# Sharing out the float64 weight roundings and the length-64 transforms over the first five channel pairs of a Fourier filter and mixer kernel

## The chip, the cores and the metric

The kernel runs on one core of one Trainium2 chip. The metric is the device time of one execution in microseconds (us), lower is better. The time of the kernel before is the median of three runs. All durations come from one profiled execution, which has its own time.

## What is computed

For a batch of 8 sequences of 3008 tokens with 256 channels, a filter in the frequency domain is followed by an MLP mixer block. Cut to what matters:

```python
X = np.fft.rfft(x, axis=1)                       # x: (8, 3008, 256)
y = np.fft.irfft(X * (filt_r + 1j * filt_i), n=3008, axis=1).astype(np.float32)
h = np.maximum(y.transpose(0, 2, 1) @ w_tok1, 0.0) @ w_tok2    # 3008 -> 256 -> 3008
u = y + h.transpose(0, 2, 1)
out = u + np.maximum(u @ w_ch1, 0.0) @ w_ch2                   # 256 -> 1536 -> 256
```

The four weight matrices arrive as float64, so the kernel rounds them to float32 itself, on the chip.

## The kernel before, in words

**The filter.** 3008 is 47 times 64. A Fourier transform of a batch is a transform of length 64 over one index (`a_unit`, one matmul of a 128x512 tile, two passes in the trace; `a_pair` with halves from the third group on) whose result goes to DRAM as z (`z_out`, L515: a ScalarE copy out of PSUM, L517, into one of two t1 buffers, and a DMA, L519), then for each of 32 frequencies a transform of length 47, the product with the filter, and the transform back (`b_pair`, `join`, `bi_pair`, L638 to L660), whose result goes to DRAM as g. The function `dft` (L535) is a generator: it works for one group of batches and stops (`yield`) after each piece. The groups are batch 0, batches 1 and 2, 3 and 4, 5 and 6, and 7. At the change from length 64 to length 47 it clears three filter tiles on GpSimd (`memset`, L664), and for the first two of 16 frequency pairs loads z back into t2 (`t2_load`, L591, on SP's DMA queue) and a table wb and the filter rows (`w_load`, L550, nine DMAs on SP's queue, L548, L215 and L217).

**The mixer.** `token_sums` and `token_relu` make the token mixer's hidden layer of a batch; `u_part` makes u for one of six tiles of 512 tokens. For each tile, `mix` (L954) loops over six channel pairs: 256 of the 1536 hidden channels. A pair's two matrix products are split into seven smaller ones each (the numbers n = 0 to 6 in the weight tiles), with sums of operands before and after. One pass i of the loop holds the first layer of pair i and the second layer of pair i-1:

- `up_first` (L840): four matmuls into PSUM (L844), a ScalarE copy into s (L847); `up_middle` (L850): two DVE adds that read that PSUM (output hh and s);
- `h_sums` of pair i-1: DVE (output t); `down` part 0: three matmuls (L878);
- the first place (`yield b, i % n, 0`);
- `up_last` (L856): three matmuls (L860) into the same PSUM banks, then two times a DVE add into hh and a ScalarE ReLU (L865);
- the second place; `down` part 1: four matmuls (L878); pieces of the next u; the third place.

Every DVE sum of the mixer carries line L822, that of the helper `v`. Both first-layer PSUM banks are used again by the next pair, so its `up_first` follows this pair's hidden adds.

At each place the loop at L1109 may advance the filter's generator of the group after this one; before the change, in group 0, it takes one piece at every place (three length-64 units a pair).

**The rounding.** A weight tile is one of 38 generators in the list `tiles`: 12 for w_tok1, 14 for w_tok2, 2 first and then 10 more for w_ch1 and w_ch2 (`LAST`, L395: c2_0, c1_1, c1_4, c2_1, c1_2, c2_2, c1_5, c2_3, c2_4, c2_5, where c1 and c2 mean `wc1_load` and `wc2_load`). Each has four steps:

1. begin: a staging tile st and its load, issued on GpSimd (L372: four DMAs; L383: one);
2. copy: ScalarE writes the upper word's float into "top" (L265);
3. middle: two DVE instructions on top (L267, L268);
4. end: two DVE instructions make "rest" (L271, L273), one or two add top and rest into the weight tile wc (L295); then `combine` (L359) makes the sums of weights, five GpSimd instructions for a pair (L362 to L366).

```python
def convert_end():
    ended[0] += 1
    advance(end)
    copies()
    fill(5)
...
    while copied[0] < len(tiles) and copied[0] <= ended[0] + (copied[0] < len(tiles) - len(LAST)):
```

`advance(it)` takes the next tile of an iterator and runs its next step. `convert` is `convert_middle` and `convert_end`. For the last ten tiles top is a tile of pool p1 and rest one of pool p2, one buffer each, so the copy of a tile follows the end of the one before it. In `mix` (L987 and L1008) there is one `convert` at the head of a pass and one after its first place. So in passes 0 to 4 the order on DVE in each half is: end of one tile, middle of the next, then the mixer's adds of that half.

**The tail.** `finish` adds up a token tile, transposes it on DVE (L910) and writes it with 16 DMAs from `store` (L925), on GpSimd's queue, but for the very last tile on three queues in turn.

Of the kernel before, what the change touches and what calls it, by code (L numbers as in the profile page):

```python
# [10 lines left out]
FP32 = mybir.dt.float32  # L11
# [12 lines left out]
P = 128  # L24
# [17 lines left out]
JP = JT // 2  # L42
# [77 lines left out]
def kernel(  # L120
# [11 lines left out]
    nc = tc.nc  # L132
# [145 lines left out]
    def spare_pair():  # L278
# [2 lines left out]
        both = where.tile([P, 2, 512], FP32, tag=tag, name="both")  # L281
        return both[:, 0], both[:, 1]

    def rounded(st, n, parts, late):
        if late:

            pair = (p1p.tile([P, 512], FP32, tag="p1", name="top"), p2p.tile([P, 512], FP32, tag="p2", name="rest"))
        else:
            pair = spare_pair()
        h = halves(st, n, pair)  # L290
        yield next(h)
        yield next(h)
        top, rest = next(h)
        for src, dst in parts:
            nc.vector.tensor_tensor(out=dst, in0=src(top), in1=src(rest), op=ALU.add)  # L295
# [115 lines left out]
    def convert():  # L411

        convert_middle()
        convert_end()

    def convert_middle():
        advance(middle)
        sum_up()

    def convert_end():  # L420
        ended[0] += 1
        advance(end)
        copies()
        fill(5)

    copied = [0]

    def copies():

        while copied[0] < len(tiles) and copied[0] <= ended[0] + (copied[0] < len(tiles) - len(LAST)):  # L430
            advance(copy)
            copied[0] += 1

# [101 lines left out]
    def dft(bs):  # L535
# [14 lines left out]
        def w_load(c):  # L550
            table_load(c)
            (filt_load if first else filt_pair)(c)
# [109 lines left out]
        for c in range(FB):  # L662
            if not first:
                nc.gpsimd.memset(filts[c][:, :, 0, :], 0.0)  # L664
            if c < 2:
                t2_load(c)
                if not first:
                    w_load(c)
        yield "w"
        yield "b"  # L670
        if not first:
# [209 lines left out]
    def finish(b, m, ut, po):  # L881

        w = width(m)
        hw = w // 2
        us = ut[:, :, 0:w].rearrange("p d (s n) -> p d s n", s=2)
        p23, p45, p16, p7 = (v_[:, :, 0:hw] for v_ in po)
        r = rp.tile([P, 512 // CW, DH, CW], FP32, tag="r", name="r")
        flat = r.rearrange("p k d i -> p (k d i)")
        p1, u2, u3 = (flat[:, ds(256 * i, hw)] for i in range(3))
        nc.scalar.copy(out=p1, in_=p16[:, 0])  # L890

        def a():
            v(us[:, 0], p23, us[:, 0])
            v(u2, p16[:, 1], p1)

        def b_():
            v(us[:, 1], p45, us[:, 1])
            v(us[:, 0, 1], p45[:, 1], us[:, 0, 1])
            v(u3, p7[:, 0], u2)

        def c():
            v(us[:, 0, 0], us[:, 0, 0], p1)
            v(us[:, 0, 1], us[:, 0, 1], u2)

        def d():
            v(us[:, 1], us[:, 1], u3.unsqueeze(1).to_broadcast([P, 2, hw]))

        def turn(dh):

            nc.vector.transpose(r[:, 0:w // CW, dh, :], ut[:, dh, 0:w].rearrange("p (k i) -> p k i", i=CW))  # L910

        def store():
            turn(1)
            ob = out[b]
            cw = DH * CW
            blocks = r.rearrange("p (q h e) d i -> p h e q (d i)", h=2, e=2)
            for h in range(2):
                n = min(4, (w - h * HALF + HALF) // P)
                for e in range(2):
                    for g in range(CB):  # L920

                        last = b == B - 1 and m == MT - 1
                        q = (nc.sync, nc.scalar, nc.gpsimd)[(h * 8 + e * 4 + g) % 3] if last else nc.gpsimd
                        row = e * 32 * N1 + (A + 4 * m if h else A - 1 - 4 * m)
                        q.dma_start(bass.AP(tensor=ob.tensor, offset=ob.offset + row * D + g * cw,  # L925
                                            ap=[[N1 * D, 32], [D if h else -D, n], [1, cw]]),
                                    blocks[ts(g, CW), h, e, 0:n])

        return [a, b_, c, d, lambda: turn(0), store]
# [3 lines left out]
    def u_part(b, m, i):  # L933
        if i == 0:
            uts[b, m] = up.tile([P, DH, 512], FP32, tag="u", name="u")
        (u_quarter if b else u_unit)(b, m, h1s[b], uts[b, m], i)
# [13 lines left out]
    def one_step():  # L950
        if todo_v:
            todo_v.pop(0)()

    def mix(next_ready):  # L954

        wait = []
        pos, hhs, tts = {}, {}, {}

        def loads(b):
            if b + 1 < B and next_ready(b):  # L960
                for c in wait:
                    t4_load(b + 1, c)
                wait.clear()


        own = ({(4, 2): (0, 1)}, {(3, 0): (0,), (4, 0): (1,), (4, 2): (2, 3)})
        new = {(JP - 2, 0): (0, 1), (JP - 1, 0): (2, 3)}

        def u_parts(b, m, jp, place):
            parts = own[b > 0] if m + 1 < MT else new if b + 1 < B else {}  # L970
            now = parts.get((jp, place), ())
            b, m = (b, m + 1) if m + 1 < MT else (b + 1, 0)
            for part in now:
                u_part(b, m, part)
            if now and now[-1] == max(p for ps in parts.values() for p in ps):
                if m:
                    wait.append(m)
                todo_v.extend(v_steps(b, m))
                if b and (b, m) < (B - 1, MT - 2):
                    w2m_load((m + 2) % MT)  # L980

        to_dram = [f for m in range(MT) for f in w2_sums(m)]
        items = [(b, m, jp) for b in range(B) for m in range(MT) for jp in range(JP)]
        n = MT * JP
        for i in range(len(items) + 1):
            now, old = i < len(items), i >= 1
            if ended[0] < len(tiles):  # L987
                convert()
            if now:
                b, m, jp = items[i]  # L990
                if i % n == 0:
                    wait.append(0)
                w = width(m)
                hhs[i] = hp.tile([P, 4, 256], FP32, tag="hh", name="hh")
                g = [bank("pg").rearrange("p (s n) -> p s n", s=2) for _ in range(2)]
                s = up_first(jp, uts[b, m], vts[b, m], w, g)
                up_middle(hhs[i], w, g, s)
            one_step()
            if old:
                bo, mo, jo = items[i - 1]  # L1000
                tts[i - 1] = tp.tile([P, 4, 256], FP32, tag="t", name="t")
                for f in h_sums(hhs[i - 1], tts[i - 1], width(mo)):
                    f()
                down(mo, jo, 0, hhs[i - 1], tts[i - 1], pos.setdefault((bo, mo), []))
            if now:
                u_parts(b, m, jp, 0)
            yield b, i % n, 0
            if ended[0] < len(tiles):  # L1008
                convert()
            if now:  # L1010
                up_last(jp, uts[b, m], vts[b, m], w, g, s, hhs[i])
            one_step()
            if now and i % n == n - 1:
                one_step()
            loads(b)
            yield b, i % n, 1
            if old:
                down(mo, jo, 1, hhs.pop(i - 1), tts.pop(i - 1), pos[bo, mo])
                if jo == JP - 1:
                    todo_v.extend(finish(bo, mo, uts[bo, mo], pos[bo, mo]))  # L1020
                    one_step()
                    one_step()
            if now:
                if b + 1 < B and i % n == n - 4:
                    h1s[b + 1] = token_relu(b + 1, token_sums(b + 1))
                u_parts(b, m, jp, 2)
                if jp == JP - 1:
                    while todo_v and m + 1 == MT:
                        one_step()
                if i >= 8 and to_dram:  # L1030
                    to_dram.pop(0)()
                if i in (28, 29):
                    w2m_load(i - 28)
            loads(b)
            yield b, i % n, 2
        while todo_v:
            one_step()

    with tc.manual_schedule():
# [53 lines left out]
        for dh in range(DH):  # L1093
            convert()
            u_part(0, 0, dh)
        for f in v_steps(0, 0):
            f()
        for _ in range(XB):
# [10 lines left out]
        for b, i, place in mix(next_ready):  # L1109
# [13 lines left out]
                due = (jp, place) in {"b": ((5, 1), (1 if i >= n - JP else 2, 1)), "m": ((0, 1), (3, 0)), "i": ((1, 0), (3, 2))}[coming]  # L1123
            else:
                due = (jp - (coming == "i")) % JP in ((5, 1, 2, 3) if i < 4 * JP else (5, 0, 1, 2, 3)) and place == {"b": 1, "m": 2, "i": 0}[coming]
            if due:
                coming = next(todo, "end")
                done = coming == "end"


# [28 lines left out]
```

## Time and profile before

| | us |
|---|---|
| median of three runs | 2480.81 (2479.5 to 2483.97) |
| profiled execution, time | 2483.14 |
| its span, first to last instruction | 2481.4 |
| TensorE busy | 2417.7 (97%) |
| VectorE (DVE) busy | 1845.1 (74%) |
| ScalarE (ACT) busy | 679.7 (27%) |
| GpSimd (POOL) busy | 598.4 (24%) |
| mean granted TensorE clock | 0.992 |

In the profile PE is the matmul part of TensorE and PEld its weight load; SP is the engine that only issues DMAs. Times in rows are us from the start of the span. A row of a timeline has start, length, engine, line, operation, output<-input, shape and count, and in brackets how long the engine sat idle before it and what released it. A name with q at its end is the engine's queue, that is the issue of a DMA. A digit of the slices is the busy share in tenths of one fortieth of the span; PEclk is the clock that was granted to TensorE.

### The profile page before, as it was taken

How to read it: one execution, taken by the hardware profiler on the slowest of the kernel's cores; microseconds unless marked ns; L12 is line 12 of the kernel's file. 1: busy time of each engine (PE TensorE's matmuls, PEld its weight loads, DVE VectorE, ACT ScalarE, POOL GpSimd, SP SyncE). 2: the span in 40 equal slices, each digit the busy share in tenths (PEclk: the TensorE clock that was granted, in tenths of full speed). 3: DMA queues.
4: the chain of work that ended last, by engine and by line, in shares of the span. 5: the costliest groups of instructions: out<-in, count | busy, mean ns of one | idle time of the engine just before them, and what ended most of it. 6: DMA issues, size and time to landing. Idle time of an engine off the chain costs nothing.

```text
span 2481.4 us, 33945 instructions
## 1 busy us (share of the span) xinstructions
PE 2417.7 (97%) x11836; PEld 1965.7 (79%) x11836; DVE 1845.1 (74%) x3404; ACT 679.7 (27%) x1348; POOL 598.4 (24%) x1086
## 2 busy tenths in 40 slices
PE   7888999999999999999999999999999999999997
PEld 3566676887878887887878877897888888898887
DVE  7686887587785878667885888758786788757776
ACT  5633232123221222223221222213221222212221
POOL 6572332211211211211121112111212112112121
PEclk8999999999999999999999999999999999999999
DMA  9973444254332222335332323313322121201100
GB/s 209 244 218 115 128 136 135 88 171 129 98 95 58 81 78 65 95 100 166 97 95 62 88 69 84 103 49 123 89 74 73 49 71 46 96 24 31 38 17 18
DMA packets 173122, 236.07 MB, mean 95 GB/s; under 512 B 33213, under 2 KB 123067, under 8 KB 172952
## 3 DMA queue, kind: packets, MB, share of 16 engines
q1 hardware_dynamic: 128344, 175.53, 24.2%
q0 software_dynamic: 33376, 48.46, 7.8%
q10 hardware_dynamic: 11232, 9.92, 1.3%
q8 instruction: 94, 1.54, 0.3%
q14 instruction: 76, 0.62, 0.1%
HBM read 156.56 MB, written 77.22 MB: 94 GB/s over the span
## 4 chain that ended last, share of the span: by engine, by line
PE 48%; DVE 2%; DMA 0%; issue 0%; ACT 0%; POOL 0%; SPq 0%; DVEq 0%; POOLq 0%; ACTq 0%
PE ps_po L878 19%; PE ps_pg L844 11%; PE ps_pg L860 8%; PE ps_acc L721 2%; PE ps_b L721 2%; PE ps_b L765 2%; PE ps_acc L765 2%; PE ps_b L501 1%; PE ps_acc L501 1%; PE ps_acc L743 1%; PE ps_b L743 1%; DVE t L822 1%; DVE hh L822 0%; DVE u L822 0%; DVE s L822 0%
## 5 line engine op out<-in xcount | busy, mean ns | idle before, releaser
L925 POOL DMA_DIRECT2D out_dram<-r x757 | 410.8, 551 | 1663.2 <-ACT hh L865 1399.6
L822 DVE TENSOR_TENSOR hh<-ps_pg,s 128x512 f32<-128x512 f32 (+3 forms) x864 | 482.6, 586 | 382.9 <-ACT s L847 380.5
L865 ACT ACTIVATE hh<-hh 128x512 f32<-128x512 f32 (+1 forms) x576 | 348.1, 621 | 960.0 <-DVE hh L822 960.0
L878 PE MATMUL ps_po<-t,wc 128*128 128x256 f32 (+1 forms) x2304 | 547.8, 381 | 4.3 <-DVE t L822 3.3
L878 PEld LDWEIGHTS ps_po<-t,wc 128*128 128x128 f32 x2304 | 427.9, 190 | 131.5 <-DVE t L822 42.7
L844 PE MATMUL ps_pg<-v,wc 128*128 128x256 f32 (+1 forms) x1728 | 415.8, 377 | 0.1
L878 PE MATMUL ps_po<-hh,wc 128*128 128x256 f32 (+1 forms) x1728 | 413.8, 376 | 0.9 <-DVE u L822 0.2
L844 PEld LDWEIGHTS ps_pg<-v,wc 128*128 128x128 f32 x1728 | 328.5, 191 | 40.9 <-DVE v L822 2.6
L878 PEld LDWEIGHTS ps_po<-hh,wc 128*128 128x128 f32 x1728 | 327.5, 190 | 41.9 <-ACT s L847 4.6
L860 PE MATMUL ps_pg<-u,wc 128*128 128x256 f32 (+1 forms) x1152 | 295.2, 379 | 5.7 <-DVE hh L822 5.7
L860 PEld LDWEIGHTS ps_pg<-u,wc 128*128 128x128 f32 x1152 | 214.9, 190 | 62.6 <-DVE hh L822 31.4
L822 DVE TENSOR_TENSOR t<-t,hh 128x256 f32<-128x256 f32 (+1 forms) x576 | 245.3, 426 | 19.8
L822 DVE TENSOR_TENSOR s<-ps_pg,hh 128x512 f32<-128x512 f32 (+1 forms) x288 | 196.1, 681 | 30.3 <-DVE hh L822 0.5
L847 ACT COPY s<-ps_pg 128x256 f32<-128x256 f32 (+1 forms) x288 | 106.0, 368 | 333.7 <-PE ps_pg L844 332.4
L822 DVE TENSOR_TENSOR t<-hh 128x512 f32<-128x512 f32 (+1 forms) x288 | 192.8, 669 | 0.6 <-ACT hh L865 0.6
L844 PE MATMUL ps_pg<-u,wc 128*128 128x256 f32 (+1 forms) x576 | 172.4, 381 | 9.3 <-DVE hh L822 9.3
L860 PE MATMUL ps_pg<-v,wc 128*128 128x256 f32 (+1 forms) x576 | 168.7, 375 | 0.0
L844 PEld LDWEIGHTS ps_pg<-u,wc 128*128 128x128 f32 x576 | 107.2, 190 | 41.5 <-DVE hh L822 26.0
L860 PEld LDWEIGHTS ps_pg<-v,wc 128*128 128x128 f32 x576 | 109.2, 190 | 12.6
L822 DVE TENSOR_TENSOR u<-ps_b,u 128x256 f32<-128x256 f32 (+2 forms) x102 | 58.3, 572 | 67.5 <-PE ps_b L765 61.8
L822 DVE TENSOR_TENSOR u<-ps_acc,u 128x512 f32<-128x512 f32 (+2 forms) x108 | 62.4, 577 | 56.5 <-PE ps_acc L765 52.2
L721 PE MATMUL ps_acc<-t,w 128*128 128x256 f32 x384 | 83.5, 379 | 0.0
(140 smaller groups left out, 2469.8 us busy)
## 6 DMA issues: line engine op xcount, KB each, us to landing
w<-w_tmp SPq DMA_DIRECT2D x35, 896.0 KB
out_dram<-r POOLq DMA_DIRECT2D x698, 32.0 KB, 2.4
t<-g_tmp SPq DMA_DIRECT2D x42, 512.0 KB
g_tmp<-t SPq DMA_DIRECT2D x96, 192.0 KB
t<-z_tmp SPq DMA_DIRECT2D x180, 96.0 KB
z_tmp<-t SPq DMA_DIRECT2D x60, 256.0 KB
filt<-in_x_dram SPq DMA_DIRECT2D x90, 128.0 KB
wb<-wbi_t SPq DMA_DIRECT2D x64, 128.0 KB
```

What stands on the lines that cost most here:

```text
L501: nc.tensor.matmul(outs(i, j), stat(i, j), mov(i, j), start=True, stop=True)
L721: nc.tensor.matmul(acc[:, t, :], w1[:, a, ts(t, P)], t4[b, a // TC4][:, a % TC4, :], start=(a == 0 and t == 0), stop=(a == A - 1 and t == ...
L743: nc.tensor.matmul(ps[:, ds(q * P, n)], t4[b, c][:, r, ts(dh, P)], wai[:, 0:n], start=(first and q == 0), stop=(not first and q == 3))
L765: nc.tensor.matmul(ps[:, ds(j * hw, hw)], h1[:, n, :], w2m[m % 2][:, at, 0:hw], start=(i < 2 and j == 0), stop=(j == len(todo) - 1))
L822: nc.vector.tensor_tensor(out=out, in0=in0, in1=in1, op=op)
L844: nc.tensor.matmul(ps[:, 0:hw], chan[0][:, jp, n, :], mov, start=True, stop=True)
L847: nc.scalar.copy(out=s[:, 0], in_=g[0][:, 0, 0:hw])
L860: nc.tensor.matmul(ps[:, 0:hw], chan[0][:, jp, n, :], mov, start=True, stop=True)
L865: nc.scalar.activation(out=hs, in_=hs, func=AF.Relu)
L878: nc.tensor.matmul(po[i][:, j, 0:hw], chan[1][:, jp, n, :], mov, start=(jp == 0 and first == 1), stop=(jp == JP - 1 and last == 1))
L925: q.dma_start(bass.AP(tensor=ob.tensor, offset=ob.offset + row * D + g * cw, ap=[[N1 * D, 32], [D if h else -D, n], [1, cw]]), blocks[ts(g ...
```

## The change

Four things, of which the first belongs to the last ten weight tiles.

- Top and rest of a tile now lie in one tile of 2x512 words, in pool p1 and pool p2 by turns. Copies are issued up to one tile ahead of the ends also for the last ten. One end step (of c2_0) is moved ahead of the mixer. In passes 1 to 4 of `mix` the head has a middle, an end and a middle; after the first place there is one end; the copies are issued ahead of the first place and after `up_last`. Pass 0 has the middle and end of c1_1 after its first place.
- In the first five passes the filter's generator gets two pieces at the first place, none at the second, one at the third.
- In `dft` the three memsets come first, and table and filter are loaded ahead of z for each of the first two frequency pairs.
- The last tile's 16 output DMAs alternate between SP's and ScalarE's queues.

```diff
+    late_in = [(p2p, "p2"), (p1p, "p1")]
...
-            pair = (p1p.tile([P, 512], FP32, tag="p1", name="top"), p2p.tile([P, 512], FP32, tag="p2", name="rest"))
+            late_in.reverse()
+            where, tag = late_in[0]
+            both = where.tile([P, 2, 512], FP32, tag=tag, name="both")
+            pair = both[:, 0], both[:, 1]
...
-    def convert_end():
+    def convert_end(copy_now=True):
         ended[0] += 1
         advance(end)
-        copies()
+        if copy_now:
+            copies()
         fill(5)
...
-        while copied[0] < len(tiles) and copied[0] <= ended[0] + (copied[0] < len(tiles) - len(LAST)):
+        while copied[0] < len(tiles) and copied[0] <= ended[0] + 1:
...
-            if c < 2:
+        if not first:
+            for c in range(2):
+                w_load(c)
                 t2_load(c)
-                if not first:
-                    w_load(c)
...
-                        q = (nc.sync, nc.scalar, nc.gpsimd)[(h * 8 + e * 4 + g) % 3] if last else nc.gpsimd
+                        q = (nc.sync, nc.scalar)[g % 2] if last else nc.gpsimd
...
-            if ended[0] < len(tiles):
-                convert()
+            if i and ended[0] < len(tiles):
+                convert_middle()
+                convert_end(False)
+                convert_middle()
...
+            if i:
+                copies()
             yield b, i % n, 0
             if ended[0] < len(tiles):
-                convert()
+                if i == 0:
+                    convert_middle()
+                convert_end(False)
             if now:
                 up_last(jp, uts[b, m], vts[b, m], w, g, s, hhs[i])
...
+            copies()
             loads(b)
             yield b, i % n, 1
...
             u_part(0, 0, dh)
+        convert_end()
...
-            if due:
-                coming = next(todo, "end")
-                done = coming == "end"
+            if coming == "a" and group == 0 and i < JP - 1:
+                due = (2, 0, 1)[place]
+            for _ in range(due):
+                if not done:
+                    coming = next(todo, "end")
+                    done = coming == "end"
```

## The prediction, made before the result was known

> **What bounds the kernel now.** I read the slices of the page first.
>
> ```profile
> PE   7888999999999999999999999999999999999997
> ...
> PEclk8999999999999999999999999999999999999999
> ```
>
> A slice is 62 us. From the fifth on, TensorE is full at full clock; only the first four and the last have room. The first mixer pairs begin at 148 us, in slices three and four. The table of stretches, cut from one pair's first L844 matmul to the next, gives pairs 1, 2, 3 and, for comparison, pair 5 (columns: stretch, length, busy time of PE, PEld, DVE, ACT, POOL, granted clock, DMA share, GB/s).
>
> ```profile
> 159.24:172.37 13.13, 10.65 (x35) 7.46 (x35) 10.39 (x19) 4.47 (x9) 10.55 (x19) 0.87 0.84 235
> 172.37:184.94 12.57, 10.57 (x34) 7.54 (x35) 9.84 (x19) 4.46 (x9) 4.68 (x9) 0.86 0.76 217
> 184.94:198.34 13.40, 9.16 (x35) 6.28 (x35) 10.67 (x19) 4.47 (x9) 9.34 (x17) 1.00 0.55 167
> ...
> 214.05:222.67 8.62, 8.62 (x35) 6.46 (x34) 5.19 (x10) 3.25 (x6) 0.00 (x0) 1.00 0.42 134
> ```
>
> With the same matmuls (28 L844/L860/L878 passes and three length-64 units), pair 5, which has no rounding, takes 8.62 us; pairs 1 to 3 take 12.6 to 13.4. DVE, with nine more instructions, is busy for 9.8 to 10.7 of that. The waits of 146 to 214 us say who waits.
>
> ```profile
> DVE top L267 <- ACT top L265: 10.1, 9, 1.6
> ...
> PE ps_pg L844 <- DVE hh L822: 9.3, 4, 2.8
> PE ps_pg L860 <- DVE hh L822: 5.7, 3, 2.7
> ```
>
> PE waits for DVE (15 us), and DVE in its turn for ScalarE's first step of a rounding. DVE's timeline over pair 2 shows where:
>
> ```profile
> 176.32 0.43 DVE L267 TENSOR_SCALAR top<-top 128x512 uint32<-128x512 uint32 x1 [1.61 <-ACT top L265]
> ...
> 182.72 0.70 DVE L267 TENSOR_SCALAR top<-top 128x512 uint32<-128x512 uint32 x1 [0.74 <-ACT top L265]
> ...
> 184.21 1.28 DVE L822 TENSOR_TENSOR hh<-ps_pg,s 128x512 f32<-128x512 f32 x2
> ```
>
> The buffer pair (p1, p2) holds one tile, so ScalarE may write the next "top" only after DVE's last add of the tile before: two round trips a pair, 0.74 and 1.6 us, both ahead of the mixer's own adds in DVE's order.
>
> **The rounding in five pairs.** Let H be the start of the two hidden-layer adds (hh, x2). Before: 158.50, 171.64, 184.21, 197.60, 208.00. The first three intervals are 13.14, 12.57, 13.39; less the two idles each they leave 10.78, 10.22, 11.03 us of DVE work, mean 10.68. Taken at the shortest durations of these rows the work is: two hidden adds 1.19, two "middle" steps at 1.07, two "end" steps 3.81, the PSUM adds 1.13, the h sums 1.52, together 9.79; the rest is stretching (L268 at 0.69 or 0.82, L822 t at 0.68 or 0.85).
>
> After the change each of pairs 1 to 4 has the same DVE work: middle and end of one tile and middle of the next ahead of the PSUM adds, the other end after the h sums. The copies are now issued half a pair ahead into the other buffer. Are they in time? In a pair of 10.7 us ScalarE runs the two ReLUs until H+1.9 (0.65 each), the second tile's copy to H+2.6, a length-64 eviction and its DMA issue (0.6+0.45), the copy of s by H+4. DVE wants that top at H+1.2+1.07+1.94 = H+4.2 and s at H+5.3. So about a microsecond and a half is left, and DVE does not wait. PE is done as well: last matmul of L860, L878 and the unit about H+0.5, next up_first H+0.7 to H+2.5. DVE then sets the period, 10.68, above PE's 8.62.
>
> Start: the added end step ahead of the mixer puts 1.94 us of DVE work ahead of the v sums, but the copy of c2_0 comes before the u eviction, so its middle starts at 143.7 instead of 145.5. v is then ready at about 149.6 against 148.6, up_first ends at 151.1 against 150.2. ScalarE holds the copy of c1_4 until its load lands (issued to 145.7, 3.8 us: 149.05 to 149.75), then two evictions at 1.05, then s at 152.2. PSUM adds 152.3 to 153.4 (before: 153.44 to 154.6), middle and end of c1_1 to 156.2: H0 = 156.2, 2.3 earlier.
>
> H4 = 156.2 + 4 x 10.68 = 198.9. The L860 matmuls of pair 4 start 3.46 us (h sums 1.52, end 1.94) ahead of H4: 195.4. From there PE has work without a gap: L860 1.29, L878 1.72, two u units 5.23, one unit 0.86, so pair 5 starts at 204.5. The same sum from 203.97 of before (plus the unit at the middle place, 0.86) gives 213.9; the trace has 214.05. **Gain 9.5 us**; with 9.79 a pair pair 5 starts at 201.0, gain 13.0. A length-64 unit moved from the middle place to the first does no work less: it fills PE while the PSUM adds run. Its eviction and z DMA on ScalarE's queue come ahead of the ReLUs, which before had one there; 1.05 us, inside the wait of ScalarE for hh (13.9 us in five). Its two t1 buffers are freed about 4 us after the issue (z DMA of 174.08, reuse 178.45), and reused every other unit: a wait of up to 0.6 at the third unit, ahead of s, is within the slack above.
>
> GpSimd: a pair with a first-layer tile has two combines (5.7 us, 161.67 to 167.38), four load issues 2.0, one combine 3.0: 10.8, equal to the period. In pair 2, down's second matmul wants the last step of c2_1: combine starts 160.3, done 166.0, loads 168.1, combine 171.1, while up_first ends at 168.3. PE waits 2.8 us there, but then has units and L860 done by 175.3, and H2 is due at 156.2+2x9.8 = 175.8 at the earliest. Covered; bare, it costs up to 3 us.
>
> **The clock.** In pairs 1 and 2 the granted clock fell to 0.50 for about 4 us each, after gaps of 2.06 and 2.48 us. The Trainium skill (TensorE: Matmul & The Clock Gate, Part 1) has the clock halved only after an idle window of some 3.4 us. By the rule these gaps cost no clock; by the rows there were two stretches, worth up to 2 us each. The rows decide, but I add nothing: pair 3 at full clock is no shorter (13.40), so the chain through DVE hid it. In the new pairs PE still has some 2 us free.
>
> **Loads at the start of the filter stage.** SP's timeline:
>
> ```profile
> 242.63 0.36 SPq L602 DMA_DIRECT2D t<-z_tmp  x1
> 243.04 0.35 SPq L548 DMA_DIRECT2D wb<-wbi_t  x1
> 243.50 0.33 SPq L215 DMA_DIRECT2D filt<-in_filt_r_dram  x1
> ```
>
> SP stood until 239.85 for z. Table and filter loads of pair 0 (nine, 3.4 us) will go ahead of that wait. b_pair starts at 245.23, 2.2 us after the table's issue; behind the last t2 load it can start 0.4 earlier. DVE's L644 stood 6.2 us for the filter until 251.0 and moves up some 3.7, but PE is behind L878 at half clock then: 0.1. **Gain 0.5**. The gap shrinks from 2.56 to 2.15. By the rule the clock would stay up and save 3.5 us (7 us at 0.50); by the rows 2.06 was enough to drop it. I take the rows: 0, and 3.5 for the far end.
>
> Groups 2 to 4 pay: there SP stands for the memset of filt (616.6 to 626.3, 1199.7 to 1209.3, 1734.9 to 1745.6), since GpSimd is behind output DMAs. The eight t2 loads, before ahead of this wait, now follow the eight filter loads: last issue about 632.1, 1215.1, 1751.4, landing 2.2 later. b_pair(0) ran at 637.22, 1220.17, 1754.55: margins 2.9, 2.9, 0.9. PE does not wait there now, so nothing can be gained. Cost 0; with a landing of 4.9 (the w load of 1218.11, the slowest near row) 1.8 in the last group alone. The loads behind (w, next t4) slip 3 us, with a dozen in hand.
>
> **The tail.**
>
> ```profile
> 2472.46 2.74 SPq L925 DMA_DIRECT2D out_dram<-r  x6
> 2472.47 2.35 ACTq L925 DMA_DIRECT2D out_dram<-r  x5
> 2472.96 2.71 POOL L925 DMA_DIRECT2D out_dram<-r  x5 [13.51 <-issue]
> ```
>
> Eight each at 0.46 to 0.47 end at 2476.2, GpSimd's five at 2475.67. The landing, 2.0 to 2.2 by these rows, is alike: **0.5 lost**. Below nothing: 0.5 gained if GpSimd's end holds the final barrier; no row tells.
>
> **Sum.** 9.5 + 0.5 - 0.5 = 9.5. The profiled execution took 2483.14 (span 2481.4 and 1.7 around it), 2.3 above the median 2480.81, so I take the difference off the median: **2471.3**. Likeliest case alone: 2468.5 to 2474.5.
>
> **Rivals.** Of no change a measurement here can tell 0.2%, 5 us: faster means below 2475.8, slower above 2485.8.
> 1. DVE sets 10.7 a pair: 2471.3. Chance 0.53.
> 2. DVE runs at 9.8, or the clock stays up at the filter stage: 2480.8 - 13.0 - 3.5 at the most, 2464.3; typically 2466. For it: half the rows are short. Against: GpSimd's steps are packed closer, and the stretched rows lie beside them. 0.16.
> 3. A new wait takes part of the old one's place: the combine in pair 2 not covered (3 us), a top waiting for its load (c2_1 issued to 154, landing 5.1, 1 us in hand), t1 held by z: 4 to 5 us lost, 2476. DMA share 0.76 to 0.84 and landings of 6.3 and 6.5 speak for it. 0.19.
> 4. The change does not uncouple: a copy still waits for the end before it through a slot I misread. Only the order differs: 2480. Against: the two tags are two pools. 0.06.
> 5. Slower: the copy at the head of ScalarE's queue. It stands ahead of two evictions and the ReLUs, and if its load has not landed all of them stand, then h sums, down and PE. Place: c2_1, c1_2, c1_5, c2_3. Slack about 3 us over landings of 4 to 5; each microsecond above 7.5 costs one per tile. It takes 15 us in four tiles to end at 2486, landings of 11; these loads showed 2.8 to 6.5. At 12 us, 2489. 0.06.
>
> Range 2464 to 2479: from case 2 to the worse half of case 3. Faster: 0.53 + 0.16 + half of case 3, less 0.02: 0.77. Slower 0.06; the rest, 0.17, within.
>
> **What would show it.** Right: no idle of DVE for "top" in pairs 1 to 4, H to H 9.8 to 11, pair 5's first L844 at 201 to 206, wb and filt issues ahead of t at 236 to 243, clock near 1.00 in pairs 1 and 2. Wrong: waits of ScalarE for st or z_tmp with DVE idle behind s (cases 3, 5); PE idle at L878 for GpSimd's wc; L501 waiting for t near 637, 1220 or 1754; a gap after H4 that gives the gain back before 242.

## The result, and the profile after

The changed kernel takes 2466.24 us (median of 4 runs, 2461.68 to 2469.55) beside 2482.39 for the kernel before in the same call (4 runs): 0.9932 of its time, 95% interval 0.9909 to 0.9955, or about 16 us less. The forecast was 2471.3, which is 9.5 us less than before, with a range of 2464 to 2479. The execution that was profiled is the slowest of the four, 2469.55 us with a span of 2467.4; against the 2481.4 of before it is 14.0 shorter. The lines of the matmuls and of the mixer's sums stand 6 lower than before: L501, L844, L860, L878 and L822 are now L507, L850, L866, L884 and L828.

Of the page's slices of TensorE's time two have changed; its clock reads as before.

```profile
PE   7889999999999999999999999999999999999998
...
PEclk8999999999999999999999999999999999999999
```

The fourth slice and the last are one step fuller. DVE's waits in pairs 0 to 4 (147 to 208 us; total, times, longest) are these, and no others:

```profile
DVE hh L828 <- PE ps_pg L866: 2.6, 1, 2.6
DVE hh L828 <- ACT s L853: 1.3, 1, 1.3
DVE s L828 <- PE ps_pg L850: 0.9, 1, 0.9
```

The row for "top" (10.1 us in nine waits before) is gone. The table of stretches has the columns of the prediction's: stretch, length, busy PE, PEld, DVE, ACT, POOL, clock, DMA share, GB/s. Its rows are pairs 0, 1, 2 and 3, and then pair 8, the first of the filter stage.

```profile
147.14:158.24 11.10, 7.46 (x21) 4.60 (x19) 8.66 (x15) 3.29 (x7) 10.19 (x19) 0.85 0.49 149
158.24:168.73 10.49, 9.30 (x35) 6.21 (x35) 10.08 (x19) 4.40 (x9) 8.12 (x14) 1.00 0.92 265
168.73:184.05 15.32, 11.98 (x34) 8.01 (x35) 12.23 (x22) 6.26 (x11) 9.99 (x17) 0.78 0.77 233
184.05:192.67 8.62, 8.62 (x36) 6.46 (x34) 8.28 (x15) 2.93 (x6) 6.55 (x11) 1.00 0.65 214
231.54:240.50 8.96, 8.73 (x37) 5.86 (x36) 7.28 (x12) 1.60 (x3) 1.70 (x4) 1.00 0.27 80
```

Pair 1 is as forecast: 10.49 us, DVE busy for 10.08 of it, clock at 1.00. Pair 2 is not: 15.32 us at a clock of 0.78. And pair 8 is 8.96 at full clock. The same stretch of the kernel before was 12.83 at 0.75:

```profile
238.19:251.02 12.83, 10.28 (x38) 7.08 (x37) 5.00 (x10) 1.60 (x4) 5.57 (x11) 0.75 0.40 119
```

TensorE's 37 or 38 matmuls there took 10.28 us and now take 8.73. To see where 14.0 us went, I cut every trace at the same marks: R, the start of the mixer's ReLUs ahead of pair 0; H0 and H4, the hidden adds of pairs 0 and 4; P5, P8 and P9, the first L844 or L850 of pairs 5, 8 and 9; and the tail, from the last matmul's end to the span's. All are differences of start times in the timelines, in us. (P5 to P8 is 24.1 in both kernels.)

| kernel | start to R | R to H0 | H0 to H4 | H4 to P5 | pair 8 | tail | span |
|---|---|---|---|---|---|---|---|
| before | 140.3 | 18.16 | 49.50 | 6.05 | 12.83 | 12.86 | 2481.4 |
| changed | 139.4 | 18.13 | 44.77 | 5.13 | 8.96 | 10.07 | 2467.4 |
| changed, once more | 137.8 | 16.86 | 43.35 | 5.13 | 9.04 | 10.09 | 2464.1 |
| roundings and units alone | 140.0 | 14.01 | 43.79 | 5.13 | 12.87 | 12.86 | 2470.3 |
| buffers alone | 142.5 | 17.37 | 44.97 | 6.04 | 11.67 | 12.87 | 2477.0 |
| load order alone | 141.1 | 17.98 | 49.48 | 6.05 | 8.84 | 12.86 | 2477.3 |
| last outputs alone | 140.0 | 18.70 | 49.49 | 6.04 | 12.41 | 10.07 | 2477.5 |
| combine later | 136.8 | 17.77 | 42.16 | 4.60 | 8.39 | 10.07 | 2460.9 |
| units as before | 139.4 | 14.38 | 42.56 | 6.04 | 10.29 | 10.08 | 2464.1 |

So in the profiled execution the pairs give 5.7 us (R to P5, forecast 9.5), the start of the filter stage 3.9 (forecast 0.5), the tail 2.8 (forecast 0.5 lost); the opening, which the change doesn't touch, was 1.0 shorter, and 0.6 lies elsewhere. The sum fell into the range for partly wrong reasons. The start to R varies from 135.6 to 142.5 among all executions of this document: 140.0 to 142.5 in the four that ran the single parts of the change, with the old roundings or the new, and 135.6 to 139.4 in the six of two later calls. No part of it is put down to the change.

### The profile page after: what moved, and what is told of

Its sections match the earlier page's. It is cut to its first block, busy times and chain, and to the rows that moved or that the text cites. A ratio compares the mean times of both kernels' runs of the same rounds, so it can differ in the third digit from the quotient of the medians.

```text
span 2467.4 us, 33933 instructions
## 1 busy us (share of the span) xinstructions
PE 2416.4 (98%) x11836; PEld 1965.0 (80%) x11836; DVE 1843.0 (75%) x3404; ACT 679.0 (28%) x1348; POOL 595.0 (24%) x1081
## 4 chain that ended last, share of the span: by engine, by line
PE 87%; DVE 6%; DMA 3%; issue 1%; POOL 1%; ACT 1%; SPq 0%; DVEq 0%; ACTq 0%; POOLq 0%
PE ps_po L884 33%; PE ps_pg L850 18%; PE ps_pg L866 14%; PE ps_acc L727 3%; PE ps_b L507 3%; PE ps_b L771 3%; PE ps_b L727 3%; PE ps_acc L771 2%; PE ps_acc L507 2%; PE ps_acc L749 2%; PE ps_b L749 2%; DMA filt<-in_filt_i_dram 1%; DVE t L828 1%; DVE hh L828 1%; DVE u L828 1%
## 5 line engine op out<-in xcount | busy, mean ns | idle before, releaser
L828 DVE TENSOR_TENSOR hh<-ps_pg,s 128x512 f32<-128x512 f32 (+3 forms) x864 | 481.8, 585 | 389.3 <-ACT s L853 382.4
L884 PE MATMUL ps_po<-t,wc 128*128 128x256 f32 (+1 forms) x2304 | 546.4, 380 | 4.5 <-DVE t L828 3.5
L884 PEld LDWEIGHTS ps_po<-t,wc 128*128 128x128 f32 x2304 | 427.0, 190 | 129.0 <-DVE t L828 43.7
L884 PE MATMUL ps_po<-hh,wc 128*128 128x256 f32 (+1 forms) x1728 | 414.7, 376 | 4.1 <-POOL wc L371 3.6
L850 PE MATMUL ps_pg<-v,wc 128*128 128x256 f32 (+1 forms) x1728 | 414.7, 376 | 2.6 <-DVE v L828 2.6
L884 PEld LDWEIGHTS ps_po<-hh,wc 128*128 128x128 f32 x1728 | 327.3, 190 | 44.9 <-POOL wc L371 4.4
L850 PEld LDWEIGHTS ps_pg<-v,wc 128*128 128x128 f32 x1728 | 328.0, 191 | 42.7 <-POOL wc L371 3.0
L866 PE MATMUL ps_pg<-u,wc 128*128 128x256 f32 (+1 forms) x1152 | 295.5, 379 | 0.0
L866 PEld LDWEIGHTS ps_pg<-u,wc 128*128 128x128 f32 x1152 | 215.7, 190 | 56.8 <-DVE hh L828 21.2
L828 DVE TENSOR_TENSOR t<-t,hh 128x256 f32<-128x256 f32 (+1 forms) x576 | 246.0, 427 | 19.8
L828 DVE TENSOR_TENSOR s<-ps_pg,hh 128x512 f32<-128x512 f32 (+1 forms) x288 | 196.0, 681 | 32.2 <-DVE hh L828 1.8
L828 DVE TENSOR_TENSOR t<-hh 128x512 f32<-128x512 f32 (+1 forms) x288 | 192.4, 668 | 0.6 <-ACT hh L871 0.6
L850 PE MATMUL ps_pg<-u,wc 128*128 128x256 f32 (+1 forms) x576 | 171.6, 379 | 2.3 <-DVE hh L828 2.3
L866 PE MATMUL ps_pg<-v,wc 128*128 128x256 f32 (+1 forms) x576 | 168.8, 375 | 0.0
L850 PEld LDWEIGHTS ps_pg<-u,wc 128*128 128x128 f32 x576 | 107.0, 190 | 33.6 <-DVE hh L828 17.8
L866 PEld LDWEIGHTS ps_pg<-v,wc 128*128 128x128 f32 x576 | 109.4, 190 | 12.5
L828 DVE TENSOR_TENSOR u<-ps_b,u 128x256 f32<-128x256 f32 (+2 forms) x102 | 58.2, 571 | 67.5 <-PE ps_b L771 61.9
L828 DVE TENSOR_TENSOR u<-ps_acc,u 128x512 f32<-128x512 f32 (+2 forms) x108 | 62.3, 577 | 55.9 <-PE ps_acc L771 51.6
L727 PE MATMUL ps_b<-t,w 128*128 128x256 f32 x384 | 83.6, 379 | 0.5 <-issue 0.5
```

The costliest lines, as they stand in the source:

```text
L727: nc.tensor.matmul(acc[:, t, :], w1[:, a, ts(t, P)], t4[b, a // TC4][:, a % TC4, :], start=(a == 0 and t == 0), stop=(a == A - 1 and t == ...
L828: nc.vector.tensor_tensor(out=out, in0=in0, in1=in1, op=op)
L850: nc.tensor.matmul(ps[:, 0:hw], chan[0][:, jp, n, :], mov, start=True, stop=True)
L866: nc.tensor.matmul(ps[:, 0:hw], chan[0][:, jp, n, :], mov, start=True, stop=True)
L884: nc.tensor.matmul(po[i][:, j, 0:hw], chan[1][:, jp, n, :], mov, start=(jp == 0 and first == 1), stop=(jp == JP - 1 and last == 1))
```

## The experiments

My theory, after the two traces were compared: four things add up, namely DVE's period in the pairs, the clock at pair 8 and the barrier at the end, less a new wait for GpSimd in pair 2. Against it stood above all that the second buffer is the whole gain in the pairs, and that a mend of the wait in pair 2 brings only the next wait; what each run should show by either stands with it.

**Last outputs on two queues, alone.** Added to the kernel before:

```diff
-                        q = (nc.sync, nc.scalar, nc.gpsimd)[(h * 8 + e * 4 + g) % 3] if last else nc.gpsimd
+                        q = (nc.sync, nc.scalar)[g % 2] if last else nc.gpsimd
```

> The kernel before with only the last 16 output DMAs on SP's and ScalarE's queues. Theory (GpSimd's queue holds the program's end): from the last matmul's end to the span's end 10.1 us as in the changed kernel, not 12.9; time 2.8 us below the kernel before, pairs and filter stage as before. Rival (the issue time of the DMAs counts, as predicted): 0.5 us slower, and the 2.8 us came from something else in the changed kernel.

2479.38 us, ratio 0.9993 (0.9984 to 1.0002): a gain of 1.7 us that its interval does not separate from none. The trace does: the tail is 10.07 instead of 12.86. GpSimd's closing instructions say why (ns min/median/max, first and last start). In the kernel before:

```profile
L1154 POOLq DRAIN  x3: 46/103/5780, 2474.8 to 2481.1; - x3
```

And in this one:

```profile
L1154 POOLq DRAIN  x2: 46/74/103, 2477.0 to 2477.3; - x2
```

In the kernel before one of GpSimd's closing DRAINs lasts 5.78 us. It begins at 2474.8 and ends 4.9 us after GpSimd's last DMA issue (2475.67), and the closing semaphore instructions of TensorE, VectorE and ScalarE start only then, at 2480.7. Without a DMA on GpSimd among the last 16 there is no such DRAIN.

**One output left on GpSimd.** The changed kernel, with only the first of the 16 transfers on GpSimd:

```diff
-                        q = (nc.sync, nc.scalar)[g % 2] if last else nc.gpsimd
+                        q = (nc.gpsimd if h + e + g == 0 else (nc.sync, nc.scalar)[g % 2]) if last else nc.gpsimd
```

> The changed kernel with one of the last 16 output DMAs, the first, on GpSimd's queue, the others on SP's and ScalarE's. Theory A (any DMA of GpSimd this near the end lengthens the program's end): last matmul to span's end 12 to 13 us, 2 to 3 us slower than the changed kernel. Theory B (only when GpSimd's last DMA is issued late does its end hold the rest): 10 to 10.5 us, time as the changed kernel.

2465.18 us, ratio 0.9926 (0.9911 to 0.9941), as the changed kernel. The long DRAIN is back among GpSimd's closing instructions, though there is but one transfer behind it:

```profile
L1171 POOLq DRAIN  x3: 46/103/5144, 2457.8 to 2463.5; - x3
```

That transfer's issue, in the timeline of the same kernel:

```profile
2457.85 0.55 POOL L931 DMA_DIRECT2D out_dram<-r  x1 [13.48 <-issue]
```

It is issued by 2458.4, and the DRAIN is done 4.6 us later. But the other queues were not done much earlier, so the tail is 10.38, 0.3 longer. So the number of transfers hardly matters: the DRAIN ends 4.6 us after the issue of one transfer and 4.9 us after that of five. It cost 0.3 us where GpSimd's issue ended 2.7 us ahead of the last one of the other queues (2458.4 and 2461.1), and 2.8 where it ended 0.5 us behind it (2475.7 and 2475.2).

**The load order alone.** The kernel before, with this edit (which leaves the memsets in a loop of their own ahead of it):

```diff
-            if c < 2:
+        if not first:
+            for c in range(2):
+                w_load(c)
                 t2_load(c)
-                if not first:
-                    w_load(c)
```

> The kernel before with only the memsets first and table and filter loaded ahead of z. Theory (b_pair stood for the table, and its first half needs only the first four z loads): pair 8 of the mixer takes about 9.0 us from first L844 to the next pair's, not 12.8, clock at 1.00 there; time 3.9 us below before. Rival (as predicted, it waits for the last z load): 12.3 us, 0.5 us below before. Second rival (the pair is short only because the earlier pairs run otherwise): 12.8 us, no gain.

2476.32 us, ratio 0.9977 (0.9968 to 0.9987): 5.7 us. Pair 8 is 8.84 at a clock of 1.00, with pairs 0 to 4 as slow as before. TensorE at pair 8 of the kernel before, its gap and the first matmuls of the mixer behind it:

```profile
245.23 1.19 PE L501 MATMUL ps_b<-t,wb 48*64 48x512 f32 x2 [2.56 <-DMA filt<-in_filt_r_dram]
...
247.44 3.78 PE L878 MATMUL ps_po<-t,wc 128*128 128x256 f32 x8
```

TensorE at pair 8 of this kernel:

```profile
243.13 1.09 PE L501 MATMUL ps_b<-t,wb 48*64 48x512 f32 x4
244.46 1.34 PE L501 MATMUL ps_acc<-t,wb 48*64 48x512 f32 x4 [0.23 <-DMA t<-z_tmp]
```

Of the old gap of 2.56 us, 0.23 is left. (The matmul reads z and the table; the row names the filter, which was loaded right behind the table.) The next run has the complement.

**Roundings and units alone.** The changed kernel with the load order and the last outputs of before.

```diff
-                        q = (nc.sync, nc.scalar)[g % 2] if last else nc.gpsimd
+                        q = (nc.sync, nc.scalar, nc.gpsimd)[(h * 8 + e * 4 + g) % 3] if last else nc.gpsimd
...
-        if not first:
-            for c in range(2):
-                w_load(c)
+            if c < 2:
                 t2_load(c)
+                if not first:
+                    w_load(c)
```

> The changed kernel without the new load order and with the old tail: roundings and length-64 units shared out anew, two buffers. Theory (the parts add up): pair 5's first L844 at 6.6 us earlier than before (5.7 of it in pairs 0 to 4), GpSimd's combine holding PE for 3.3 us in pair 2, then nothing more: pair 8 at 12.3 to 12.8 us; time 5.5 to 7 below before. Rival (the parts need one another): another 3 us or more at pair 8 without the new order.

2472.1 us, ratio 0.9964 (0.9951 to 0.9977): 8.9 us. R to P5 is 62.9, 10.8 less than before and more than I expected, since here DVE was not behind at the start and TensorE did not wait for v. Pair 8 is 12.87 again, and the waits around it (total, times, longest) name the table:

```profile
PE ps_b L507 <- DMA wb<-wbi_t: 2.5, 1, 2.5
```

The three parts measured apart give 8.9 + 5.7 + 1.7 = 16.3 us; the whole change gives 16.9 by its ratio (0.0068 of 2482.39) and 16.1 by the medians. They add up, as far as intervals of 2 to 3 us either way on each part, and of 5.5 on the whole, can tell.

**The second buffer alone.** The kernel before with the pair of tiles and the copies one tile ahead, steps and units at their old places:

```diff
+    late_in = [(p2p, "p2"), (p1p, "p1")]
...
+            late_in.reverse()
+            where, tag = late_in[0]
+            both = where.tile([P, 2, 512], FP32, tag=tag, name="both")
+            pair = both[:, 0], both[:, 1]
...
-        while copied[0] < len(tiles) and copied[0] <= ended[0] + (copied[0] < len(tiles) - len(LAST)):
+        while copied[0] < len(tiles) and copied[0] <= ended[0] + 1:
```

> The kernel before with two buffers for the last ten weight tiles and copies up to one tile ahead, but the steps at their old places (a middle and an end at the head of a pass and after its first place) and the length-64 units as before. Theory (the round trip over ScalarE was the wait): no idle of DVE for top in pairs 1 to 3, which take 10.2 to 11 us of DVE each, pair 5 starts 5 to 9 us earlier than before; time 5 to 9 below before. Rival (the new sharing over the halves does it): pairs stay at 12.5 to 13.4, less than 2 us gained.

2476.67 us, ratio 0.9976 (0.9967 to 0.9986): 6.0 us. DVE's waits for "top" are gone with the buffers alone, and H0 to H4 is 44.97 instead of 49.50. The first three intervals between hidden adds are 11.5 to 12.0 us, not 10.5, because of a new wait (pairs 0 to 4, total, times, longest):

```profile
ACT both L265 <- DVE wc L300: 23.2, 7, 6.0
...
DVE hh L827 <- ACT s L852: 4.8, 4, 1.8
```

ScalarE's copy into the second buffer stands in ScalarE's queue until DVE's end step frees that buffer, and ScalarE's copy of s stands behind it. With the steps at their new places the wait for s is 1.3 us, once, in the changed kernel. So the buffers give 4.5 of the 5.7 us that H0 to H4 gains in the run above, and the new sharing 1.2; H4 to P5 and what lies ahead of H0 come on top, and in the same call the times are 6.0 and 8.9 us less.

**Units as before.** The changed kernel without its two lines for `due`, one unit at each place:

```diff
-            if coming == "a" and group == 0 and i < JP - 1:
-                due = (2, 0, 1)[place]
```

> The changed kernel with the length-64 units one at each place, as before. Theory (a unit moved to the first place fills PE only while it waits for the PSUM adds): pair 5 starts within 1 us of the changed kernel's, time the same within 1 us. Rival (the move is part of the gain): each of pairs 1 to 4 is 0.9 us longer, 3 us in all.

2462.46 us, ratio 0.9923 (0.9909 to 0.9936): no difference from the changed kernel that can be measured. In the trace the moved unit saves 0.9 us once, between H4 and P5 (6.04 against 5.13). This trace has something else to show, at pair 8: 10.29 us at a clock of 0.87, although the longest wait of TensorE there is 0.30 us.

```profile
226.53:236.83 10.30, 10.00 (x38) 6.69 (x36) 8.51 (x13) 1.60 (x4) 3.03 (x6) 0.87 0.34 97
```

```profile
232.32 1.42 PE L507 MATMUL ps_acc<-t,wb 48*64 48x512 f32 x4 [0.30 <-DMA t<-z_tmp]
233.67 3.37 PE L884 MATMUL ps_po<-t,wc 128*128 128x256 f32 x8
```

The last row takes 1.99 at full clock in the changed kernel. Of the eight traces with the new load order, the other seven have pair 8 at 8.4 to 9.1 us and full clock.

**The changed kernel once more**, to see what comes again:

> The changed kernel once more, unaltered, beside the two others. Theory: the wait for the combine in pair 2 (3.3 us) and H0 to H4 of 44.8 us come again, since they follow from the order; v 6.8 to 9.3 us after the ReLU and H0 14 to 18, since these follow from the state of the opening. Rival (the 3.3 us was chance): no wait for wc over 1 us.

2464.15 us, ratio 0.9927 (0.9914 to 0.994). The wait in pair 2 came again, 3.4 us, and with a different price. Here is TensorE's timeline at that place in the changed kernel as first profiled (start, length, and in brackets the wait):

```profile
174.49 2.08 PE L884 MATMUL ps_po<-hh,wc 128*128 128x256 f32 x4 [3.33 <-POOL wc L371]
176.35 1.92 PE L514 MATMUL ps_acc<-filt,wa 128*128 128x512 f32 x2
178.06 1.92 PE L514 MATMUL ps_b<-filt,wa 128*128 128x512 f32 x2
```

The same place in the changed kernel, once more:

```profile
171.83 2.08 PE L884 MATMUL ps_po<-hh,wc 128*128 128x256 f32 x4 [3.44 <-POOL wc L371]
173.70 1.54 PE L514 MATMUL ps_acc<-filt,wa 128*128 128x512 f32 x2
175.08 1.02 PE L514 MATMUL ps_b<-filt,wa 128*128 128x512 f32 x2
```

And in the kernel with the units as before:

```profile
170.85 1.13 PE L884 MATMUL ps_po<-hh,wc 128*128 128x256 f32 x4 [3.34 <-POOL wc L371]
171.82 1.02 PE L514 MATMUL ps_acc<-filt,wa 128*128 128x512 f32 x2
```

A unit takes 1.02 at full clock and 1.92 at half (a granted clock of 0.50 from 175 to 179 us of the first trace). After nearly the same gap the clock was low for over 5 us, for some 3, and not at all, and the interval between hidden adds was 13.24, 11.77 and 10.56. Three other kernels with the gap (3.44 or 3.45) fit in: 12.05, 13.05 and 13.18, the first with the shorter dip. So where the clock stayed up the gap was covered. But the kernel with the units as before has one unit (0.86 us) less ahead of L866 than the others; that the gap alone would be covered in the changed kernel too is worked out below, not seen. The rest of its price is the clock behind it.

**The wait in pair 2 mended.** The changed kernel, with the second of two combines of a first-layer tile put behind the next combine of the second layer:

```diff
-            for jp in range(2 * q, 2 * q + 2):
-                combine(chan[0][:, jp:jp + 1])
+            combine(chan[0][:, 2 * q:2 * q + 1])
+            put_off.append(2 * q + 1)
...
+        while put_off:
+            jp = put_off.pop()
+            combine(chan[0][:, jp:jp + 1])
```

> The changed kernel, in which a first-layer tile's second combine (the odd pair's weights) is put behind the combine of the next second-layer tile. Theory (in pair 2 PE stands 3.3 us for GpSimd's chain of two combines, a load and a third combine, and then runs at half clock): c2_1 is combined some 3 us earlier, the wait for wc at pair 2 is under 0.5, pair 2 takes 10 to 11.5 us rather than 15.3, pair 5 starts at 202.5 to 204.5, time 3 to 5 below the changed kernel. Rival (GpSimd hides another wait of DVE's): the wait goes, but H to H stays, less than 1 us gained.

The mend does what it should. Pair 2, in this kernel's table of stretches:

```profile
165.29:175.84 10.55, 9.52 (x34) 6.07 (x34) 10.14 (x19) 4.45 (x10) 7.86 (x12) 1.00 0.82 256
```

H0 to H4 is 42.16, which is 2.6 and 1.2 less than in the two traces of the changed kernel. The 3 to 5 us in time did not show: 2464.49 us, ratio 0.9927 (0.9914 to 0.9939), is not to be told from the changed kernel's.

**The end step of c2_0 behind the PSUM adds.** The changed kernel, with `convert_end()` taken from ahead of the v sums and put into pass 0 of `mix`:

```diff
+                if i == 0:
+                    convert_end()
...
-        convert_end()
```

> The changed kernel in which the end step that it moved ahead of the mixer (c2_0) runs behind the PSUM adds of pair 0 instead of ahead of the v sums. Theory (in an execution whose VectorE is late at the token mixer's ReLU, that end step delays v and with it pair 0 by up to 2.5 us): v starts 6.8 us after the ReLU as in the kernel before, PE does not wait for v, and the first hidden adds H0 come 15 to 15.5 us after the ReLU in every execution (the changed kernel: 14.0 to 18.1). Time within 2 us of the changed kernel. Rival (only the late loads of the opening set H0): H0 varies as before, up to 18.

Half as expected. TensorE no longer waits for v (from R to v 6.79 us, as before; 9.26 in the changed kernel's profile), but R to H0 is 16.74, not 15 to 15.5: the step's 2.1 us on DVE now lie between the PSUM adds and H0 instead. 2464.94 us, ratio 0.9933 (0.992 to 0.9945).

**Both mends.**

> The changed kernel with that end step behind pair 0's PSUM adds and with the second combine of a first-layer tile put off. Theory (two small waits are left in the changed kernel, 2.6 us at the combine in pair 2 and up to 2.5 at v): H0 15 to 15.5 us after the ReLU, H0 to H4 42.2, pair 5 62 to 63 us after the ReLU (changed kernel 68.0); time 2 to 5 us below the changed kernel run beside it. Rival (what is taken off there comes back at the next wait): H0 to H4 over 44.

The wait moved. The first-layer weights of pairs 0 and 1 are now combined too late, 1.4 us in pair 0 and 1.5 in pair 1; the waits of pairs 0 to 4 have this row:

```profile
PE ps_pg L855 <- POOL wc L370: 2.9, 2, 1.5
```

And pair 1 in the table of stretches of the same kernel:

```profile
153.63:166.88 13.25, 11.74 (x34) 8.40 (x35) 12.59 (x22) 6.14 (x11) 12.56 (x23) 0.74 0.64 185
```

R to H0 is 17.28 (expected 15 to 15.5), R to P5 65.5 (expected 62 to 63), H0 to H4 43.63, and the time 2464.56 us, ratio 0.9931 (0.9918 to 0.9943). GpSimd is busy for 12.56 of these 13.25 us and DVE for 12.59, so in this pair neither has room. That GpSimd is the next limit of the whole stage is likely, but not shown. No version beat the changed kernel by what can be measured.

## Why the prediction was right, and where it was wrong

**DVE's period: right.** "DVE then sets the period, 10.68". In the two traces of the changed kernel the intervals between hidden adds are 10.49 to 10.54 us outside pair 2, with DVE busy for 10.08 in pair 1. The waits for "top" are gone, as the forecast's list asked; the 9.8 of rival 2 did not come.

**Pair 2's combine: the step that failed inside the pairs' 9.5.** "PE waits 2.8 us there ... Covered; bare, it costs up to 3 us." The wait came in the place that was named, at 3.33. GpSimd's chain in the changed kernel, the start and end of the two combines and of the third:

```profile
161.86 0.62 POOL L367 TENSOR_SCALAR wc<-wc 128x128 f32<-128x128 f32 x1 [1.89 <-DVE wc L300]
...
167.87 0.52 POOL L371 TENSOR_TENSOR wc<-wc 128x128 f32<-128x128 f32 x1
...
170.43 0.79 POOL L367 TENSOR_SCALAR wc<-wc 128x128 f32<-128x128 f32 x1
...
173.65 0.78 POOL L371 TENSOR_TENSOR wc<-wc 128x128 f32<-128x128 f32 x1
```

It began at 161.86 (forecast 160.3). The two combines took 6.5 us, not 5.7, and the combine of c2_1 took 4.0 (170.43 to 174.43), not 3.0. The 5.7 was also a misreading of the kernel before, where 167.38 is the start of the last operation and not the end:

```profile
167.38 0.52 POOL L366 TENSOR_TENSOR wc<-wc 128x128 f32<-128x128 f32 x1
```

By the durations at full clock it would still have been covered: from 174.49 four matmuls (0.9), two units (1.7) and L866 (1.3) end at 178.4, and DVE was ready at 178.64. What was left out was the clock: "The rows decide, but I add nothing". At half clock the same work ended 2.6 us after DVE was ready, and H2 came 2.7 late:

```profile
181.24 1.29 DVE L828 TENSOR_TENSOR hh<-ps_pg,s 128x512 f32<-128x512 f32 x2 [2.60 <-PE ps_pg L866]
```

The reason for adding nothing, that "in the new pairs PE still has some 2 us free", doesn't hold behind a gap that has already used them.

**The start: forecast 2.3 earlier at H0; between 0 and 4.2 seen.** "v is then ready at about 149.6 against 148.6". The added end step did delay v where DVE was behind at R: TensorE waited 2.58 us for v in the changed kernel's profile, at half clock after it, and R to H0 gained nothing. Where DVE was not behind, in two traces, there was no wait, and R to H0 fell to 14.0 and 14.4. The others lie between. Which of these happens seems to hang on the opening; that is argued from these executions and was not set by an experiment. By this and the clock, R to P5 gains 5.7, 8.1, 8.4 and 10.8 in four traces with the same roundings and units; the timed 8.9 is near the forecast 9.5.

**The load order: mis-sized, 0.5 for 3.9 in the trace and 5.7 in time.** "behind the last t2 load it can start 0.4 earlier". The mechanism, table and filter ahead of z, was right. But b_pair's first four matmul passes need only the first half of the t2 loads. Of SP's timeline in the changed kernel, the first and the last of those eight issues:

```profile
233.04 0.30 SPq L607 DMA_DIRECT2D t<-z_tmp  x1
235.82 0.37 SPq L608 DMA_DIRECT2D t<-z_tmp  x1
```

And TensorE's, at the same time:

```profile
235.95 1.13 PE L507 MATMUL ps_b<-t,wb 48*64 48x512 f32 x4
237.31 1.43 PE L507 MATMUL ps_acc<-t,wb 48*64 48x512 f32 x4 [0.23 <-DMA t<-z_tmp]
```

The last load is being issued at 235.82, and TensorE begins at 235.95 with no gap at all; the second half finds its load 1.5 us after the last issue began, not 2.2 after it. The remaining gap of 2.15, and with it the row of 2.06 that decided against the clock, never arose. Of the 3.9 us, 2.3 are the gap and 1.6 are busy time of TensorE at full clock instead of half. So the clock that stays up, which was kept for the far end of the range, was the likely case. In groups 2 to 4 the later t2 loads cost nothing, as forecast: no matmul at L507 waits for t there.

**The tail: wrong in sign, 0.5 lost for 2.8 gained in the trace.** "The landing ... is alike" compared issues and landings, and the issues were as worked out. What ends the span in the kernel before is GpSimd's DRAIN, 5.7 us before the end at its last issue, against 2.3 us from the last issue on SP or ScalarE to the end of the span. The prediction named it ("if GpSimd's end holds the final barrier; no row tells") but priced it at 0.5. A row did tell: the closing line of the kernel before, shown under the first experiment, which the prediction left out.

**The sum.** Forecast 9.5 + 0.5 - 0.5; in the trace 5.7 + 3.9 + 2.8, where the errors partly cancel; timed parts 8.9 + 5.7 + 1.7, where the excess over the forecast is the load order and the tail. That the range held owes something to luck: it had the clock at pair 8 only as a rare case, and the tail's gain hardly at all. The measured total lies nearest to rival 2's 2466, and by the second of its two ways; rival 3's combine came true as well, at 2.7 us where it counted 4 to 5 for its waits together.

## What to carry to other kernels

A gap of TensorE can cost twice, by its length and by the matmuls behind it at half clock; whether a wait is "covered" has to be reckoned with both. Ask of each wait which of several loads the first instruction needs, not when the last has landed. And look at the closing lines of a trace before moving the last stores: the end of a program has waits of its own, and here late DMAs of GpSimd held it for 2.8 us.

## What the runs showed of the hardware

- The length of a gap alone does not tell the clock behind it. TensorE idle for 3.33 to 3.45 us brought a low clock for some 3 to 5 us in five executions and none in one; a gap of 2.58 brought it (pair 0 of the changed kernel), and so did two of 1.67 and 1.51 close together (pair 1 of the last kernel, 0.74). Gaps of 2.73 and 2.76 in the kernel before, and one of 3.01 in the kernel with the load order alone, did not. And once the clock fell with no wait above 0.30 us ahead of it (pair 8 with the units as before, 0.87), which no run explains. The Trainium skill (TensorE: Matmul & The Clock Gate, Part 1) has the clock set by an activity window of about 3.4 us that runs freely, and takes from it that gaps above some 3.4 us are the ones to avoid. A free phase would fit the scatter, though no row here shows the window; that only gaps above 3.4 us count does not fit these rows. By the page's rule the gap of 3.33 in the changed kernel would cost its length alone; the low clock behind it made H2 2.7 us later.
- GpSimd's closing DRAIN lasted until 4.6 us after its last DMA issue with one transfer near the end, and until 4.9 us after it with five.
- A combine of the same five GpSimd operations took 2.5 to 4.0 us in these traces, which made 3.0 a poor figure for a margin of less than a microsecond.
